# A three-part transformer block on one core: small TensorE operations set singly behind the large matmuls of the next step

## The chip, the cores and the metric

One core of a Trainium2 chip runs the whole program. The metric is the device time of one execution in microseconds (us). The kernel before took 716.36 us, the median of three runs (715.81 to 716.93).

## The reference, cut to what matters

Four batches of 576 positions (2304 tokens in all) go through a windowed attention with eight heads of 64 (four heads see the last 32 positions, four see every fourth of the last 128), then a gated feed-forward layer 512 to 1536 to 512 with an RMS norm ahead, then a second layer 512 to 1024 to 512 with a softmax-weighted activation and a layer norm between its two products.

```python
scores = np.where(masks, scale * q @ k.T, -1e9)
attn = softmax(scores);  x = attn @ v                    # tokens x 512
rms = np.sqrt(np.mean(x * x, axis=-1, keepdims=True) + 1e-06)
xn = x / rms * rms_g
g = xn @ w_gate;  x = (silu(g) * (xn @ w_val)) @ w_out   # 512 -> 1536 -> 512
h = x @ w_in                                             # 512 -> 1024
solu = h * softmax(h)
ln = (solu - mu) / np.sqrt(var + 1e-06) * g_ln
out = ln @ w_out2                                        # 1024 -> 512
```

## The kernel before

**Numbers.** Each operand of a large product is split into a high and a low part, and one product is three matmuls (high by high, high by low, low by high) that add up in PSUM: `mm3` (L909), `product` inside `joint` (L1250), `p_product` (L1565) and `p_products` (L1637). Such a matmul has a stationary side of 128 by 128, loaded by a weight load of its own, and a moving side of 512 columns (256 for one part of the tokens). They are called the large ones here.

**Stages.** The tokens are cut into nine tiles of 256, the tiles into five parts. Attention works through units (one or two groups of heads of a tile): scores, masking, maximum, exponential, sum, division, transposes, the product with v. A unit's 2 or 4 transposes (L662; line L531 for the four earliest units, which the change leaves as they are) turn the weights on TensorE: the data are the stationary side, an identity of 128 columns is the moving side, and the result lands in PSUM, tile `tp`. ScalarE copies it out twice, masked (`turned`, tile `pT`). The mean of the squares for the RMS norm (`mean`, emitted by `total`, L807) is, for the seven later tiles, two matmuls with a moving side of one column; each of these shows in the trace as two. Between all this run the products of the first layer (`g`, `vp`, `out`). From about 315 us the last two parts are done together in Strassen form (`joint`: m1 to m7). From about 500 us the second layer runs, pair r of token tiles by pair: its first product as seven sub-products p1 to p7 (`pair_steps`), then per token tile i of 128 the activation and norm, eight transposes in two sets of four (`p_t`, L1626, PSUM tile `tp`, one bank per set), their split into high and low (`p_lt`: ScalarE casts each set into `lt`, L320; VectorE subtracts, L329), and the product with w_out2 in two halves of twelve matmuls (`p_products`, L1645 to L1647, PSUM tile `o`).

**What sets the order.** Every step is registered with `plan.add`: its engines with an assumed cost, what it needs, what it occupies, and a due time. A list scheduler (`Plan.order`) plays the steps in assumed time and returns one order; the program is emitted in it, so every engine's queue is that list filtered by engine. In the second layer TensorE's order is written out by hand (`line` in `second_stage`): o of tile a first half, transposes of tile b, o of a second half, p2, p7, p4 of the next pair, o of b first half, p3, transposes of the next a, o of b second half, p1, p5, p6 of the pair after. The product p6 adds onto the bank in which p1 left its result, after that result has been copied out (`kept("s1", "p1")`, a copy by ScalarE or VectorE into `h` or `he`). `put` (L318) is the helper behind all copies and casts, `less` (L328) behind all subtractions.

Of the kernel before, what the change touches and what calls it, by code (L numbers as in the profile page):

```python
# [20 lines left out]
P = 128  # L21
KD = DM // P
NF1 = FF1 // P
NF2 = FF2 // P
# [150 lines left out]
    return [("cl" if t == X_ELSEWHERE else "x", x_key(t))]  # L175


class Plan:


# [92 lines left out]
def tile_attention_glu_solu(ctx: ExitStack, tc: tile.TileContext, qk_d, v_d, w1_d, win2_d, wout2_d,  # L273
                            rmsg_d, gln_d, mask_d, ident_d, out):
    nc = tc.nc
# [17 lines left out]
    ident = const.tile([P, P], F32, name="ident")  # L293
# [4 lines left out]
    ones = const.tile([P, P], F32, name="ones")  # L298
# [11 lines left out]
    T = {}  # L310
# [28 lines left out]
                             seed.to_broadcast([P, x.shape[1]]), start=not add, stop=not add)  # L339

    w1 = {}

# [241 lines left out]
    def attention(t, m, due, needs):  # L586
# [3 lines left out]
        g, at_ = gs[0], PLACE[t, ns[0]]  # L590
        K = (t, m)
        w = 512 + g["nk"]
# [64 lines left out]
        def transposes(e):  # L657

            x = new_bank(tp, [P, 4, P], "tp")
            fill(x.rearrange("p u q -> p (u q)"))  # L660
            for u in range(2 * N):
                nc.tensor.transpose(x[:, u], T[s_][:, 2 * u:2 * u + 2, :].rearrange("p r k -> p (r k)"), ident)  # L662

        def turned(r):

# [88 lines left out]
    def rms(t, due, first):  # L754
        p, i = PART_OF[t]
# [45 lines left out]
        def total(k):  # L801

            def emit(e):
                if k == ks[0]:
                    bank(a_mean, [P, 2], "ms")
                for c in range(2):
                    nc.tensor.matmul(T[a_mean][:, c:c + 1], T["sq", t, k][:, P * c:P * c + P], ones[:, 0:1],  # L807
                                     start=k == ks[0] and c == 0 if first else True,
                                     stop=k == ks[-1] and c == 1 if first else True)
            return emit  # L810

        def eps(e):
# [94 lines left out]


    def mm3(acc, wh, wl, xh, xl, first, last):  # L909
        nc.tensor.matmul(acc, wh, xh, start=first, stop=False)  # L910
        nc.tensor.matmul(acc, wh, xl, start=False, stop=False)  # L911
        nc.tensor.matmul(acc, wl, xh, start=False, stop=last)  # L912

    def mlp(v, due):
        p, c0, n, fs = VIRTUAL[v]
# [132 lines left out]
    def joint():  # L1048
# [107 lines left out]
        def group_(q):  # L1156
# [88 lines left out]
            def product(name, a, b, x, more, needs):  # L1245
                def emit(e):
                    for j in range(2):
                        (wh, wl), xu = left(a, j), x_unit(b, j)
                        for n, (w, y) in enumerate(((wh, xu[:, 0]), (wh, xu[:, 1]), (wl, xu[:, 0]))):
                            nc.tensor.matmul(acc(x), w, y, start=not more and j == 0 and n == 0, stop=j == 1 and n == 2,  # L1250
                                             skip_group_check=True)
                add((name, q), {"t": 6 * mm}, emit, needs + lows(b) + ([("slow", q)] if a[0] == "s" else []) +
                    [made[1, f, X] for f in fs], takes=[] if more else [(tag_of[x], bank[x])],
                    uses=[bank[x]] + ([shl] if a[0] == "s" else []) + ([("xt4",)] if b == "t4" else []), due=7000)
# [310 lines left out]
    def p_product(r, a, b, bank, more):  # L1565
        o, yh = p_bank(r, bank), pairs[r]
        for j in range(2):
            x = LEFT[a]
            w = w_in[b, j]
            first, last_ = j == 0 and not more, j == 1  # L1570
            hi = yh[0][x > 2][:, x - 3 * (x > 2), j]
            nc.tensor.matmul(o, hi, w[:, 0], start=first, stop=False, skip_group_check=True)
            nc.tensor.matmul(o, hi, w[:, 1], start=False, stop=False, skip_group_check=True)
            nc.tensor.matmul(o, yh[1][:, x, j], w[:, 0], start=False, stop=last_, skip_group_check=True)

    def p_sum(r, row, col, kept, bank, n):
        if n == 0:
# [42 lines left out]
    def p_t(i, q):  # L1620
        e = flat(p_row(i // 2, ("e", i % 2)))
        tag, n = plan.where["tp", i, q]
        tp = tp_of[i, q] = psy.tile([P, HALF, P], F32, tag=f"{tag}{n}", name="tp")
        for k in range(HALF):
            c = (q * HALF + k) * P
            nc.tensor.transpose(tp[:, k, :], e[:, c:c + P], ident)  # L1626

    def p_lt(i, q, h, e):
        if i not in lt_of:
# [7 lines left out]
    def p_products(i, ks, a=0, n=DM):  # L1637
        lt = lt_of[i]
        if (i, a) not in o_of:
            tag, x = plan.where["o", i, a]  # L1640
            o_of[i, a] = psy.tile([P, 512], F32, tag=f"{tag}{x}", name="o")[:, 0:n]
        o = o_of[i, a]
        for k in ks:
            w = w1[OUT_AT[k]][:, :, a:a + n]
            nc.tensor.matmul(o, lt[:, 0, k], w[:, 0], start=(k == 0), stop=False)  # L1645
            nc.tensor.matmul(o, lt[:, 0, k], w[:, 1], start=False, stop=False)  # L1646
            nc.tensor.matmul(o, lt[:, 1, k], w[:, 0], start=False, stop=(k == NF2 - 1))  # L1647

    rows = [(PIECES[t][j][0] * S + PIECES[t][j][1], PIECES[t][j][2])
            for p in PARTS for t in p for j in range(len(PIECES[t]))]  # L1650
# [180 lines left out]
    nc.scalar.activation(early, mhalf[:, 0:1], AF.Exp)  # L1831
    with tc.manual_schedule():
        free, warm = 0.0, ps.tile([P, TP], F32, tag="vp0", name="warm")
        for at_, _, name, e in plan.play():
            if e == "t":
                filling[0] = int((at_ - free) / (0.13 if free else 0.25)) if at_ < FILL else 0
                free = at_ + plan.steps[name]["engines"]["t"]
                if name[0] == "spread":
                    warm = None
                if warm is not None:  # L1840
                    fill(warm)
            plan.steps[name]["emit"](e)


def _layout(q, k, v):
# [69 lines left out]
```

## Time and profile before

| | |
|---|---|
| median of three runs | 716.36 us |
| the profiled execution | 717.14 us, of which the profile's span is 715.1 us |
| TensorE busy | 706.7 us (99% of the span) |
| TensorE weight loads | 597.1 us (83%) |
| VectorE, ScalarE, GpSimd busy | 485.6, 361.8, 125.7 us |
| granted TensorE clock, mean | 0.997 |

The span runs from the first to the last recorded instruction; 2.0 us of the profiled execution lie outside it. PE is TensorE's matmuls, PEld its weight loads, DVE is VectorE, ACT is ScalarE. A matmul's recorded length holds its way through the array, so matmuls that follow closely overlap in the record: what a matmul costs the queue is the distance from its start to the next one's, not its length.

### The profile page before, as it was taken

To read this page: it belongs to the slowest core of one execution; us is meant where nothing else is said; L and a number is where in the kernel's file an instruction comes from. 1 tells how busy PE (TensorE), PEld (TensorE's weight loads), DVE (VectorE), ACT (ScalarE), POOL (GpSimd) and SP (SyncE) were. 2 spreads that over 40 slices of the span, in tenths; PEclk is the share of its full clock that TensorE was granted. 3 is DMA by queue.
4 is the path that set the end of the run, shared out by engine and by line. 5 is a ranking of instruction groups with operands and counts; after the bars stand their busy time and mean duration, and the time that the engine had idled before them with its cause. 6 is when DMAs were issued, how large, how long until landed. Compare 5 with 4: busy or idle time off the path is not lost.

```text
span 715.1 us, 11752 instructions
## 1 busy us (share of the span) xinstructions
PE 706.7 (99%) x4561; PEld 597.1 (83%) x4561; DVE 485.6 (68%) x891; ACT 361.8 (51%) x775; POOL 125.7 (18%) x159
## 2 busy tenths in 40 slices
PE   8999999999999999999999999999999999999998
PEld 5788888899998888888888888888778888888887
DVE  4798897478657665367766666689677676665552
ACT  2877835354435563335555554355365555443440
POOL 0323033232312211110000000014044411001110
PEclk9999999999999999999999999999999999999999
DMA  9999323173278837204211112846032111000001
GB/s 325 402 408 345 135 85 136 60 235 125 103 257 296 290 118 215 94 30 143 93 44 44 60 58 91 321 161 223 0 118 74 59 61 45 29 16 31 29 30 45
DMA packets 42423, 97.22 MB, mean 136 GB/s; under 512 B 3840, under 2 KB 14080, under 8 KB 42368
## 3 DMA queue, kind: packets, MB, share of 16 engines
q1 hardware_dynamic: 40640, 93.33, 37.4%
q10 hardware_dynamic: 1728, 3.15, 1.2%
q8 instruction: 36, 0.59, 0.4%
q14 instruction: 19, 0.16, 0.1%
HBM read 72.87 MB, written 23.59 MB: 135 GB/s over the span
## 4 chain that ended last, share of the span: by engine, by line
PE 88%; DVE 4%; DMA 4%; issue 1%; ACT 1%; POOL 1%; SPq 1%; DVEq 0%; ACTq 0%; POOLq 0%
PE ca L1250 7%; PE y L910 5%; PE y L912 5%; PE y L911 5%; PE o L1647 5%; PE o L1645 5%; PE o L1646 5%; PE g L910 4%; PE vp L910 4%; PE g L911 4%; PE vp L912 4%; PE g L912 4%; PE vp L911 4%; PE pv L682 2%; PE cd L1250 2%; PE cc L1250 2%
## 5 line engine op out<-in xcount | busy, mean ns | idle before, releaser
L1645 PE MATMUL o<-w,lt 128*128 128x512 f32 (+1 forms) x152 | 58.9, 388 | 0.0
L1647 PE MATMUL o<-w,lt 128*128 128x512 f32 (+1 forms) x152 | 57.6, 379 | 0.0
L1646 PE MATMUL o<-w,lt 128*128 128x512 f32 (+1 forms) x152 | 57.5, 379 | 0.0
L329 POOL TENSOR_TENSOR w<-wf,w 128x512 fp32r<-128x512 f32 (+1 forms) x12 | 19.8, 1658 | 196.4 <-ACT w L320 196.4
L910 PE MATMUL y<-uh,w 128*128 128x512 f32 (+1 forms) x148 | 53.7, 363 | 0.0
L912 PE MATMUL y<-uh,w 128*128 128x512 f32 (+1 forms) x148 | 51.8, 350 | 0.0
L911 PE MATMUL y<-uh,w 128*128 128x512 f32 (+1 forms) x148 | 51.7, 349 | 0.0
L647 ACT ACTIVATE s<-s,nm 128x64 f32<-128x64 f32 x120 | 40.1, 336 | 20.4 <-DVE nm L642 20.4
L944 ACT ACTIVATE u<-g 128x512 f32<-128x512 f32 (+1 forms) x37 | 19.1, 516 | 46.6 <-PE g L912 46.5
L792 POOL TENSOR_TENSOR sq<-x 128x256 f32<-128x256 f32 x28 | 19.7, 713 | 127.2 <-DVE x L324 65.4
L910 PE MATMUL g<-xh,w 128*128 128x512 f32 (+1 forms) x104 | 40.6, 390 | 0.0
L910 PE MATMUL vp<-xh,w 128*128 128x512 f32 (+1 forms) x100 | 39.4, 394 | 0.0
L320 ACT CAST w<-wf 128x512 fp32r<-128x512 f32 (+1 forms) x40 | 28.3, 727 | 21.2 <-DVE wf L382 8.8
L911 PE MATMUL g<-xl,w 128*128 128x512 f32 (+1 forms) x104 | 38.9, 374 | 0.0
L912 PE MATMUL g<-xh,w 128*128 128x512 f32 (+1 forms) x104 | 38.9, 374 | 0.0
L912 PE MATMUL vp<-xh,w 128*128 128x512 f32 (+1 forms) x100 | 38.2, 382 | 0.0
L911 PE MATMUL vp<-xl,w 128*128 128x512 f32 (+1 forms) x100 | 38.1, 381 | 0.0
L954 DVE SCALAR_TENSOR_TENSOR u<-u,vp 128x512 f32<-128x512 f32 (+1 forms) x37 | 21.7, 586 | 22.2 <-PE vp L912 21.4
L320 ACT CAST uh<-u 128x512 fp32r<-128x512 f32 (+1 forms) x37 | 19.8, 536 | 28.8 <-DVE u L954 28.5
L950 DVE SCALAR_TENSOR_TENSOR u<-u,g 128x512 f32<-128x512 f32 (+1 forms) x37 | 21.6, 584 | 17.5 <-ACT u L944 17.1
L1647 PEld LDWEIGHTS o<-w,lt 128*128 128x128 f32 x152 | 28.6, 188 | 5.4
L1645 PEld LDWEIGHTS o<-w,lt 128*128 128x128 f32 x152 | 28.6, 188 | 4.8
(284 smaller groups left out, 2017.8 us busy)
## 6 DMA issues: line engine op xcount, KB each, us to landing
raw<-w SPq DMA_DIRECT2D x36, 512.0 KB, 9.1
es<-ec SPq DMA_DIRECT2D x12, 512.0 KB, 3.3
sc<-es SPq DMA_DIRECT2D x12, 512.0 KB, 3.3
qk<-qk SPq DMA_DIRECT2D x7, 800.0 KB, 5.9
vt<-v SPq DMA_DIRECT2D x10, 512.0 KB, 5.1
wo<-w SPq DMA_DIRECT2D x9, 512.0 KB, 8.6
wst<-wo SPq DMA_DIRECT2D x9, 512.0 KB, 3.7
yT<-yo SPq DMA_DIRECT2D x16, 256.0 KB, 3.5
```

The source lines that it names most:

```text
L320: nc.scalar.copy(dst, src) if scale is None else nc.scalar.mul(dst, src, scale)
L329: ENG[e].tensor_tensor(dst, a, b, ALU.subtract)
L647: nc.scalar.activation(T[s_][:, i], T[s_][:, i], AF.Exp, bias=st["nm"][:, i:i + 1], accum_out=sm[:, i:i + 1])
L910: nc.tensor.matmul(acc, wh, xh, start=first, stop=False)
L911: nc.tensor.matmul(acc, wh, xl, start=False, stop=False)
L912: nc.tensor.matmul(acc, wl, xh, start=False, stop=last)
L950: return lambda e: nc.vector.scalar_tensor_tensor(out=u_of(f), in0=u_of(f), scalar=1.0, in1=T["g", v, f], op0=ALU.add, op1=ALU.mult)
L954: return lambda e: nc.vector.scalar_tensor_tensor(out=u_of(f), in0=u_of(f), scalar=0.5, in1=T["vp", v, f], op0=ALU.mult, op1=ALU.mult)
L1250: nc.tensor.matmul(acc(x), w, y, start=not more and j == 0 and n == 0, stop=j == 1 and n == 2, skip_group_check=True)
L1645: nc.tensor.matmul(o, lt[:, 0, k], w[:, 0], start=(k == 0), stop=False)
L1646: nc.tensor.matmul(o, lt[:, 0, k], w[:, 1], start=False, stop=False)
L1647: nc.tensor.matmul(o, lt[:, 1, k], w[:, 0], start=False, stop=(k == NF2 - 1))
```

## The change

A transpose step and a mean step no longer issue their matmuls. They put them on a list (`small_ones`), and each large matmul of the next TensorE step takes one from the list and issues it right behind itself (`large`). What is left at the end of that step is issued then (`flush`). Only the steps named in `LARGE` take small ones; ahead of any other TensorE step the list is emptied. When a step of another engine that needs a listed step comes up in the plan's order first, the next TensorE step is pulled ahead of it, or, if that step isn't a large one or isn't ready, the list is emptied. The plan itself, its costs and due times are as before.

```diff
--- before
+++ changed
@@ -175,6 +175,10 @@
     return [("cl" if t == X_ELSEWHERE else "x", x_key(t))]
+WEAVE = ("t", "transposes", "mean")
+LARGE = ("g", "vp", "out", "o") + tuple(f"{x}{n}" for x in "mp" for n in range(1, 8))
+
+
 class Plan:
@@ -340,6 +344,21 @@
+    pending, woven = [], set()
+
+    def small_ones(*fs):
+        pending.extend(fs)
+
+    def flush():
+        while pending:
+            pending.pop(0)()
+        woven.clear()
+
+    def large(*args, **more):
+        nc.tensor.matmul(*args, **more)
+        if pending:
+            pending.pop(0)()
+
     w1 = {}
     def prepare(stage, f, cuts, srcs, scales, dues, needs=(), lead=((1, 0), "joined", 0)):
@@ -659,7 +678,8 @@
             x = new_bank(tp, [P, 4, P], "tp")
             fill(x.rearrange("p u q -> p (u q)"))
             for u in range(2 * N):
-                nc.tensor.transpose(x[:, u], T[s_][:, 2 * u:2 * u + 2, :].rearrange("p r k -> p (r k)"), ident)
+                y = T[s_][:, 2 * u:2 * u + 2, :].rearrange("p r k -> p (r k)")
+                small_ones(lambda u=u, y=y: nc.tensor.transpose(x[:, u], y, ident))
         def turned(r):
@@ -804,9 +824,11 @@
                 if k == ks[0]:
                     bank(a_mean, [P, 2], "ms")
                 for c in range(2):
-                    nc.tensor.matmul(T[a_mean][:, c:c + 1], T["sq", t, k][:, P * c:P * c + P], ones[:, 0:1],
-                                     start=k == ks[0] and c == 0 if first else True,
-                                     stop=k == ks[-1] and c == 1 if first else True)
+                    x, y = T[a_mean][:, c:c + 1], T["sq", t, k][:, P * c:P * c + P]
+                    if first:
+                        nc.tensor.matmul(x, y, ones[:, 0:1], start=k == ks[0] and c == 0, stop=k == ks[-1] and c == 1)
+                    else:
+                        small_ones(lambda x=x, y=y: nc.tensor.matmul(x, y, ones[:, 0:1], start=True, stop=True))
             return emit
         def eps(e):
@@ -907,9 +929,9 @@
     def mm3(acc, wh, wl, xh, xl, first, last):
-        nc.tensor.matmul(acc, wh, xh, start=first, stop=False)
-        nc.tensor.matmul(acc, wh, xl, start=False, stop=False)
-        nc.tensor.matmul(acc, wl, xh, start=False, stop=last)
+        large(acc, wh, xh, start=first, stop=False)
+        large(acc, wh, xl, start=False, stop=False)
+        large(acc, wl, xh, start=False, stop=last)
     def mlp(v, due):
         p, c0, n, fs = VIRTUAL[v]
...
@@ -1569,9 +1591,9 @@
             w = w_in[b, j]
             first, last_ = j == 0 and not more, j == 1
             hi = yh[0][x > 2][:, x - 3 * (x > 2), j]
-            nc.tensor.matmul(o, hi, w[:, 0], start=first, stop=False, skip_group_check=True)
-            nc.tensor.matmul(o, hi, w[:, 1], start=False, stop=False, skip_group_check=True)
-            nc.tensor.matmul(o, yh[1][:, x, j], w[:, 0], start=False, stop=last_, skip_group_check=True)
+            large(o, hi, w[:, 0], start=first, stop=False, skip_group_check=True)
+            large(o, hi, w[:, 1], start=False, stop=False, skip_group_check=True)
+            large(o, yh[1][:, x, j], w[:, 0], start=False, stop=last_, skip_group_check=True)
     def p_sum(r, row, col, kept, bank, n):
         if n == 0:
@@ -1623,7 +1645,7 @@
         tp = tp_of[i, q] = psy.tile([P, HALF, P], F32, tag=f"{tag}{n}", name="tp")
         for k in range(HALF):
             c = (q * HALF + k) * P
-            nc.tensor.transpose(tp[:, k, :], e[:, c:c + P], ident)
+            small_ones(lambda k=k, c=c: nc.tensor.transpose(tp[:, k, :], e[:, c:c + P], ident))
     def p_lt(i, q, h, e):
         if i not in lt_of:
...
@@ -1831,7 +1853,20 @@
     nc.scalar.activation(early, mhalf[:, 0:1], AF.Exp)
     with tc.manual_schedule():
         free, warm = 0.0, ps.tile([P, TP], F32, tag="vp0", name="warm")
-        for at_, _, name, e in plan.play():
+        todo, emitted = plan.play(), set()
+
+        def needs_of(name):
+            return set(plan.steps[name]["needs"])
+
+        while todo:
+            at_, _, name, e = todo[0]
+            if woven & (needs_of(name) - plan.steps[name]["after"]):
+                at_, _, name, e = next(y for y in todo if y[3] == "t")
+                if name[0] not in WEAVE + LARGE or needs_of(name) - emitted:
+                    flush()
+                    at_, _, name, e = todo[0]
+            todo.remove(next(y for y in todo if y[2] == name))
+            emitted.add(name)
             if e == "t":
                 filling[0] = int((at_ - free) / (0.13 if free else 0.25)) if at_ < FILL else 0
                 free = at_ + plan.steps[name]["engines"]["t"]
@@ -1839,7 +1874,13 @@
                     warm = None
                 if warm is not None:
                     fill(warm)
+                if name[0] not in WEAVE + LARGE:
+                    flush()
             plan.steps[name]["emit"](e)
+            if e == "t" and name[0] in WEAVE and pending:
+                woven.add(name)
+            elif e == "t":
+                flush()
 def _layout(q, k, v):
```

The order of VectorE, ScalarE, GpSimd and the DMA queue stays what it was, row for row. On TensorE the 204 transposes of L662 and L1626 and the 14 mean matmuls stood in runs of 2, 4 or 8; of them 201 transposes and all 14 means now stand singly behind a large matmul (187 and 10 behind one with 512 columns, the rest behind one with 256), and one run of three transposes is left.

TensorE in the second layer, before: the eight transposes (`tp`, two banks) of one token tile stand between p3 of a pair (`hb`) and the second half of o of the tile ahead.

```order
L1574 MATMUL hb_5398<-w0_1_449,yh_5291 128x512
L1626 MATMUL tp_5489<-ident_83,e_5304 128x128 x4
L1626 MATMUL tp_5496<-ident_83,e_5304 128x128 x4
L1645 MATMUL o_5457<-w3_2_875,lt_5366 128x512
L1646 MATMUL o_5457<-w3_2_875,lt_5366 128x512
L1647 MATMUL o_5457<-w3_2_875,lt_5366 128x512
L1645 MATMUL o_5457<-w6_1_1060,lt_5366 128x512
```

The same place in the changed kernel, from the last matmuls of p3 on (line L358 is now the one line of all large matmuls, L1648 the transposes).

```order
L358 MATMUL hb_5398<-w0_1_449,yh_5291 128x512 x3
L358 MATMUL o_5457<-w3_2_871,lt_5378 128x512
L1648 MATMUL tp_5489<-ident_83,e_5296 128x128
L358 MATMUL o_5457<-w3_2_871,lt_5378 128x512
L1648 MATMUL tp_5489<-ident_83,e_5296 128x128
L358 MATMUL o_5457<-w3_2_871,lt_5378 128x512
L1648 MATMUL tp_5489<-ident_83,e_5296 128x128
L358 MATMUL o_5457<-w6_1_1060,lt_5378 128x512
L1648 MATMUL tp_5489<-ident_83,e_5296 128x128
L358 MATMUL o_5457<-w6_1_1060,lt_5378 128x512
L1648 MATMUL tp_5492<-ident_83,e_5296 128x128
L358 MATMUL o_5457<-w6_1_1060,lt_5378 128x512
```

The transposes of the second bank now start behind the fifth large matmul of the half, and the last of them stands behind the eighth of its twelve.

ScalarE at this place, in the changed kernel: `lt` are the two casts of the transposed sets, `yh` a cast for the next pair, `sq` a square of the norm, `ob` the scaled result of an earlier tile, `h` the copy of p1's result (and after it one more).

```order
L324 CAST yh_5490<-y_5394 128x768
L324 CAST lt_5514<-tp_5489 128x512
L324 CAST lt_5514<-tp_5492 128x512
L324 CAST yh_5490<-y_5394 128x1024
L1626 ACTIVATE sq_5523,st_5317<-e_5296,st_5317 128x1024
L324 ACTIVATE ob_5533<-o_5457,st_5156 128x512
L324 COPY h_5545<-ha_5525 128x512 x2
```

Nothing moved here: the kernel before has the same rows in the same order (its helper is line L320, its square L1604).

TensorE at the mean of one tile in the first layer, before: `ms` are the two mean matmuls, in front of the second half of a `vp` product.

```order
L912 MATMUL vp_1344<-xh_460,w9_0_1258 128x512
L807 MATMUL ms_1352<-ones_88,sq_970 128x1 x2
L910 MATMUL vp_1344<-xh_460,w9_0_1258 128x512
L911 MATMUL vp_1344<-xl_465,w9_0_1258 128x512
L912 MATMUL vp_1344<-xh_460,w9_0_1258 128x512
```

And in the changed kernel.

```order
L358 MATMUL vp_1344<-xh_460,w9_0_1258 128x512 x2
L831 MATMUL ms_1352<-ones_88,sq_970 128x1
L358 MATMUL vp_1344<-xl_465,w9_0_1258 128x512
L831 MATMUL ms_1352<-ones_88,sq_970 128x1
L358 MATMUL vp_1344<-xh_460,w9_0_1258 128x512 x2
```

The two means are one large matmul apart, and the first stands one large matmul later than it did.

## Rows read from the trace of the kernel before

**Rows 1.** The page's first part (busy time, share, instructions) and its clock row.

```profile
PE 706.7 (99%) x4561; PEld 597.1 (83%) x4561; DVE 485.6 (68%) x891; ACT 361.8 (51%) x775; POOL 125.7 (18%) x159
...
PEclk9999999999999999999999999999999999999999
```

**Rows 2.** Groups by line and shape on PE: busy us, mean ns of one.

```profile
L1626 PE MATMUL tp<-ident,he 128*128 128x128 f32 x80 | 10.4, 272 | 0.0
...
L662 PE MATMUL tp<-ident,s 128*128 128x128 f32 x60 | 9.2, 273 | 0.0
L1626 PE MATMUL tp<-ident,e 128*128 128x128 f32 x64 | 8.3, 272 | 0.0
```

**Rows 3.** Timeline of PE, one run of eight transposes: start, length, instruction.

```profile
560.31 0.40 PE L1647 MATMUL o<-w,lt 128*128 128x512 f32 x1
560.55 1.04 PE L1626 MATMUL tp<-ident,e 128*128 128x128 f32 x8
561.34 0.48 PE L1645 MATMUL o<-w,lt 128*128 128x512 f32 x1
561.65 0.40 PE L1646 MATMUL o<-w,lt 128*128 128x512 f32 x1
...
562.34 0.39 PE L1646 MATMUL o<-w,lt 128*128 128x512 f32 x1
...
565.97 0.39 PE L1574 MATMUL ha<-w,yl 128*128 128x512 f32 x1
```

**Rows 4.** Timeline of the weight loads in the same stretch.

```profile
560.31 1.03 PEld L1626 LDWEIGHTS tp<-ident,e 128*128 128x128 f32 x8
561.31 0.19 PEld L1645 LDWEIGHTS o<-w,lt 128*128 128x128 f32 x1
561.42 0.19 PEld L1646 LDWEIGHTS o<-w,lt 128*128 128x128 f32 x1
```

**Rows 5.** Timeline of PE, a run of four transposes in the first layer.

```profile
105.67 0.39 PE L912 MATMUL vp<-xh,w 128*128 128x512 f32 x1
105.90 0.60 PE L662 MATMUL tp<-ident,s 128*128 128x128 f32 x4
```

**Rows 6.** Timeline of PE, the matmuls of one mean.

```profile
116.77 0.50 PE L807 MATMUL ms<-ones,sq 128*128 128x1 f32 x4
```

**Rows 7.** Timeline of the weight loads behind that mean.

```profile
117.11 0.19 PEld L910 LDWEIGHTS vp<-xh,w 128*128 128x128 f32 x1
```

**Rows 8.** Timeline of PE, large matmuls with 256 columns.

```profile
162.97 0.28 PE L910 MATMUL y<-uh,w 128*128 128x256 f32 x1
...
163.57 0.28 PE L912 MATMUL y<-uh,w 128*128 128x256 f32 x1
```

**Rows 9.** Timeline of PE, one turn of the second layer: transposes, then p6's first matmul.

```profile
550.13 1.03 PE L1626 MATMUL tp<-ident,e 128*128 128x128 f32 x8
...
556.46 0.39 PE L1572 MATMUL ha<-w,w 128*128 128x512 f32 x1
```

**Rows 10.** Timeline of ACT in that turn; in brackets its idle time and what ended it.

```profile
551.11 1.07 ACT L320 CAST lt<-tp 128x512 fp32r<-128x512 f32 x2
...
554.16 0.69 ACT L320 ACTIVATE ob<-o,st 128x512 f32<-128x512 f32 x1
555.29 0.59 ACT L320 COPY h<-ha 128x512 f32<-128x512 f32 x1 [0.45 <-PE ha L1574]
```

**Rows 11.** Timeline of PE, the transposes of the last such turn.

```profile
661.13 1.04 PE L1626 MATMUL tp<-ident,he 128*128 128x128 f32 x8
```

**Rows 12.** Timeline of ACT in the last such turn.

```profile
661.76 1.07 ACT L320 CAST lt<-tp 128x512 fp32r<-128x512 f32 x2 [2.20 <-PE tp L1626]
...
666.29 0.59 ACT L320 COPY he<-ha 128x512 f32<-128x512 f32 x1 [0.61 <-PE ha L1574]
```

**Rows 13.** Timeline of ACT, the copies of one attention unit.

```profile
140.09 1.27 ACT L320 ACTIVATE pT<-tp,half 128x512 f32<-128x512 f32 x2 [0.46 <-PE tp L662]
```

**Rows 14.** Timeline of PE, that unit's product with v.

```profile
142.07 1.15 PE L682 MATMUL pv<-pT,vt 128*64 128x64 f32 x32
```

More of the change, by code (lines that the diff above doesn't have):

```diff
@@ L1249, in emit @@
                         for n, (w, y) in enumerate(((wh, xu[:, 0]), (wh, xu[:, 1]), (wl, xu[:, 0]))):
-                            nc.tensor.matmul(acc(x), w, y, start=not more and j == 0 and n == 0, stop=j == 1 and n == 2,
+                            large(acc(x), w, y, start=not more and j == 0 and n == 0, stop=j == 1 and n == 2,
                                              skip_group_check=True)
@@ L1644, in p_products @@
             w = w1[OUT_AT[k]][:, :, a:a + n]
-            nc.tensor.matmul(o, lt[:, 0, k], w[:, 0], start=(k == 0), stop=False)
-            nc.tensor.matmul(o, lt[:, 0, k], w[:, 1], start=False, stop=False)
-            nc.tensor.matmul(o, lt[:, 1, k], w[:, 0], start=False, stop=(k == NF2 - 1))
+            large(o, lt[:, 0, k], w[:, 0], start=(k == 0), stop=False)
+            large(o, lt[:, 0, k], w[:, 1], start=False, stop=False)
+            large(o, lt[:, 1, k], w[:, 0], start=False, stop=(k == NF2 - 1))
     rows = [(PIECES[t][j][0] * S + PIECES[t][j][1], PIECES[t][j][2])
```

## The prediction

> **What bounds the kernel now.** I read the page's first part and its clock row first, then the groups by line on TensorE, then the timeline around runs of transposes, matmuls and weight loads apart, and last the timeline of ScalarE behind them. TensorE's matmuls are busy 99% of the span, and the granted clock is full in almost every slice (the higher of its two levels, 2.4 GHz) [rows 1]. So the kernel's time is the sum of what its matmuls cost TensorE's queue, and a change pays if that sum gets smaller or a wait of TensorE goes. The operations moved are 144 transposes in the second layer and 60 in attention [rows 2], and 14 mean matmuls. By the groups they look dear (272 ns each), but that is a recorded length, and what counts is the distance between starts.
>
> That distance is read at a run of eight [rows 3]. Large matmuls follow each other 0.227 us apart (562.34 to 565.97, 16 steps). From the large one ahead of the run (560.31) to the fifth behind it (562.34) pass 2.03 us; five steps without transposes would be 1.13. So eight transposes cost 0.90 us, 0.112 each. The weight loads show why [rows 4]: a load starts when the matmul just ahead of it starts, never earlier, and the load of the first large matmul behind the run starts at 561.31, with the eighth transpose; the next load, which marks that large matmul's true start, comes at 561.42. Eight transposes from 560.55 to 561.31 are seven steps of 0.109, and from the last one to the large matmul there are again 0.11.
>
> The means tell what the 0.11 is [rows 6, 7]: four matmuls that stream one column still stand 0.113 apart (116.77 to 117.11, three steps). Where nothing streams, the load alone sets the step, some 0.11 us. A large matmul hides the load behind it; a short one doesn't.
>
> The Trainium skill, in "TensorE: Matmul & The Clock Gate", section "Step-by-step: what each phase is for", says that TensorE's queue pulls weight loads ahead of matmuls in flight, with the matmuls in order. Here the trace agrees so far as one load ahead, and shows none two matmuls ahead.
>
> **The transposes.** In the changed kernel a pair is large, transpose, large. Its two gaps both occur in the trace already. Large to transpose is 0.24 in the second layer [rows 3] and 0.23 in attention [rows 5]; transpose to large is 0.11 [rows 4]. The transpose's own load is now always hidden, but the load of the next large matmul is always exposed: in a run of eight there are eight exposed loads (seven transposes' and one large one's), and singly there are eight exposed loads of large ones. Together 0.34 to 0.35 less the 0.227 of the large one: 0.113 to 0.123 per transpose, against 0.112. At the upper end the slightly longer step after a run (561.42 to 561.65 is 0.23) now comes every time, 0.005 more: 0.128. At the lower end a switch costs nothing, 0.227 + 0.109, so 0.109. So per transpose between 0.003 less and 0.016 more, times 201: -0.6 to +3.2 us. I take the middle, 0.006 more, since both switch distances were measured above the plain step: +1.2 us. The means have the same balance; two runs of two in place of one of four pay the switch twice, about 0.03 us for each of seven tiles: +0.2.
>
> **What becomes late.** A transpose set is ready later, because large matmuls stand between its members. In the second layer the queue behind that is ScalarE's, and its order is unchanged: two casts of the set, a cast for the next pair, a square, a scaled result, and then the copy of p1's result, for which p6 on TensorE waits. Before, the eight transposes begin at 550.13 [rows 9] and the last is done at 550.13 + 0.76 + 0.27, 551.16; ScalarE starts the first cast at 551.11 and the second half a length later, at about 551.6 [rows 10]. Now the large matmul takes the place at 550.13, the first transpose follows at 550.36, the eighth seven pairs of 0.34 later at 552.75, done at 553.03. The second cast starts at 553.1, 1.5 us later, and everything behind it on ScalarE with it. The cover is ScalarE's idle time ahead of the copy, 0.45 us, and the distance from the copy's end, 555.88, to p6's start at 556.46, 0.58 [rows 9, 10]: 1.03 in all. So p6 starts some 0.5 us late and TensorE stands still for that long. In the last such turn the transposes begin at 661.13 [rows 11], so the eighth is done at 664.03; the second cast stood at about 662.25, is 1.8 late, and finds 0.61 idle and the same 0.58 ahead of p6 [rows 12]: 0.6. There are six such turns, 22.2 us apart (550.13 to 661.13 are five of them) [rows 9, 11]; in five the copy is ScalarE's, in one VectorE's, whose queue I find covered. Five times 0.5 to 0.65 is 2.7 us. Bounds: if a part of the delay is made up, 0.2 each, 1 us; if each wait is 0.9, as when the whole 1.5 meets only the 0.58, 4.5 us. I take 2.7, since its terms are single rows.
>
> In attention a unit's fourth transpose ends some 0.9 us later in a stream of 512 columns (three more large matmuls and one ahead), half of that with 256. The copies behind it [rows 13] end at 141.36 and the product with v starts at 142.07 [rows 14], 0.71 ahead; the other units are alike or wider. That gives a wait of a few tenths in two or three units. Against it, a transpose now waits for its input one large matmul later, which saves as much where VectorE is the late one. I cost this at +0.1 us, between -0.4 and +1.
>
> Nothing moves on the DMA queues or on GpSimd, and no wait of another engine is added.
>
> **The sum.** 1.2 + 0.2 + 2.7 + 0.1 = 4.2 us. The profiled execution of before took 717.1 us, its span 715.1 with 2.0 around it; it would become 721.3. The median of the runs is 0.8 below the profiled one, so the forecast is 716.4 + 4.2, about 720.5 us.
>
> **The rivals.**
> First, the small ones dearer singly. A run of eight pays 0.90 - 8 x 0.109, about 0.025 us, beyond its steps; if every transpose pays all of that by itself, each costs 0.021 more than now, 201 of them 4.2 us, and with the waits (3.0) the time is 723.6. For it: the step is longer for more than one large matmul after a run. Against it: in the new order the next transpose comes before those later steps.
>
> Second, the waits don't come: ScalarE gains the delay back between the second cast and the copy. Then only the 1.2 + 0.2 stay, 717.8 us. For it: ScalarE is busy only 51% [rows 1]. Against it: in these turns it is idle only 0.45 to 0.61 us behind the casts [rows 10, 12].
>
> Third, on the other side: the transpose hides. If 0.109 in a run is the transposes' own loading, and behind a large matmul a transpose occupies the array only for its columns, it costs little. Large matmuls with 256 columns stand 0.12 apart (162.97 to 163.57, five steps) [rows 8] and with 512 columns 0.227, so 128 columns are worth 0.053 and a transpose 0.053 + 0.013, 0.066: 0.046 less than now, 201 times, 9.2 us saved, against 3.0 of waits: 710.2 us. The point from which it decides is the gap from a transpose to the large matmul behind it: below about 0.095 us the kernel gets faster in spite of the waits. That gap stands in the trace, at the end of every run, at 0.11, and the means show a load alone at the same size.
>
> The Trainium skill's page "TensorE: Matmul & The Clock Gate", section "Back-to-back issue gap", speaks for this rival: 128 columns at full clock cost 56 ns back to back. By that, as an estimate, the saving would be 201 x 0.056 = 11 us and the time about 708. The trace differs: runs stand at 109 ns.
>
> That the change doesn't do what it says is excluded by the order: only three of 204 transposes are left in a run.
>
> **How the numbers follow.** The forecast (waits at p6, small switches) gets 62%, with its own range 719 to 722.5; the first rival 15%, the second 16%, the third 7%. The range reaches from just below the second rival to the first: 717.3 to 723.6. 0.2% of 716.4 is 1.4 us, about what a measurement of this kernel can tell from no change: faster is under 714.9, slower over 717.8. The second rival sits on that edge; I give 11% to the same and 7% to faster, the rest, 82%, to slower.
>
> **What would show it.** In the profile after: transposes singly, 0.34 to 0.35 us from large to large across one; a load ahead of the next large matmul that starts with the transpose. ScalarE's second cast of a set 1.5 to 1.8 us later within its turn, no idle time ahead of the copy of p1's result in five turns, and PE idle of about 0.5 us at p6 (`ha`) waiting for ScalarE, where before it has none. It would be wrong if large-to-large across a transpose is under 0.32 us, or if p6 starts without a wait.

## The result, and the profile after

The kernel became slower by 0.7%: 721.90 us, the median of 6 runs, against 716.44 for the kernel before on the same chip; the ratio is 1.0069, with a 95% interval of 1.0057 to 1.0080. The profiled execution took 722.4 us and its span is 720.4, against 717.1 and 715.1 before: 5.3 us more. Nearly all of it lies on TensorE's queue, whose last matmul starts 5.2 us later than before. First the page's opening part, which answers to [rows 1]:

```profile
PE 711.3 (99%) x4561; PEld 593.6 (82%) x4561; DVE 487.8 (68%) x891; ACT 361.8 (50%) x775; POOL 125.0 (17%) x159
...
PEclk9999999999999999999999999999999999999999
```

The groups by line and shape on TensorE that answer to [rows 2] (last columns: busy us, mean ns of one, idle time ahead):

```profile
L1648 PE MATMUL tp<-ident,he 128*128 128x128 f32 x80 | 21.3, 271 | 0.0
L1648 PE MATMUL tp<-ident,e 128*128 128x128 f32 x64 | 17.3, 271 | 0.0
L682 PE MATMUL tp<-ident,s 128*128 128x128 f32 x60 | 15.9, 271 | 0.0
```

The instructions are as many as before and the granted clock is full. The transposes' busy time doubles (10.4 to 21.3 us in the first group) while the mean of one stays 271 ns: alone, a transpose's recorded length no longer overlaps that of the next one. That is why the cost isn't read from this column, but from the starts. The timeline of TensorE in the turn of [rows 9]:

```profile
551.68 0.39 PE L358 MATMUL o<-w,lt 128*128 128x512 f32 x1
551.92 0.27 PE L1648 MATMUL tp<-ident,e 128*128 128x128 f32 x1
551.94 0.48 PE L358 MATMUL o<-w,lt 128*128 128x512 f32 x1
552.26 0.27 PE L1648 MATMUL tp<-ident,e 128*128 128x128 f32 x1
...
554.33 0.27 PE L1648 MATMUL tp<-ident,e 128*128 128x128 f32 x1
554.36 1.17 PE L358 MATMUL o<-w,lt 128*128 128x512 f32 x4
555.36 0.62 PE L358 MATMUL ha<-w,w 128*128 128x512 f32 x2
...
557.86 0.39 PE L358 MATMUL hb<-w,yl 128*128 128x512 f32 x1
558.42 0.73 PE L358 MATMUL ha<-w,w 128*128 128x512 f32 x2 [0.18 <-ACT h L324]
558.99 0.40 PE L358 MATMUL ha<-w,yl 128*128 128x512 f32 x1
```

Transposes stand 0.345 us apart (551.92 to 554.33, seven steps), one large matmul between each two: 0.118 more than the plain step of 0.227. From 551.68 to 555.36 are twelve large steps and eight transposes, 3.68 - 12 x 0.227 = 0.96 for the set, against 0.90 in [rows 3]. Counted up to the twelfth large matmul behind each set it is 0.97 in thirteen of the eighteen sets, and 0.94 to 1.02 in the others.

At 558.42 stands what the forecast named: p6's first matmul waits for ScalarE's copy `h`. From 557.86 it stands 0.56 behind, where 0.227 is the step, and the next step is 0.34 (the first two are one row; the third, at 558.99, is 0.57 behind the first, and 0.23 of that is its own step): 0.33 + 0.11 lost. The timeline of ScalarE there answers to [rows 10]:

```profile
553.27 0.59 ACT L324 CAST lt<-tp 128x512 fp32r<-128x512 f32 x1 [0.51 <-PE tp L1648]
554.64 0.59 ACT L324 CAST lt<-tp 128x512 fp32r<-128x512 f32 x1 [0.78 <-PE tp L1648]
...
557.22 0.68 ACT L324 ACTIVATE ob<-o,st 128x512 f32<-128x512 f32 x1
557.79 0.58 ACT L324 COPY h<-ha 128x512 f32<-128x512 f32 x1
```

The two casts, back to back before, now each wait for TensorE, and the 0.45 idle ahead of the copy is gone. Such a wait stands in five turns (558.42, 603.59, 626.38, 649.17, 672.14), 0.42 to 0.45 us in four of them and 0.6 in the last: 2.3 in all.

In attention the jump is at one unit. First TensorE's timeline, where the product with v answers to [rows 14], then SyncE's queue of loads (`pv` is the product with v, `sp` the scores, `rs` a matmul that spreads the factors of the norm over the partitions and needs VectorE's `rd`):

```profile
142.66 1.15 PE L702 MATMUL pv<-pT,vt 128*64 128x64 f32 x32 [0.17 <-ACT pT L324]
...
151.95 1.15 PE L645 MATMUL sp<-qk 128*64 128x64 f32 x32 [0.54 <-DMA qk<-qk]
...
154.91 0.67 PE L849 MATMUL rs<-rd,ones 128*128 128x256 f32 x2 [0.19 <-DVE rd L844]
```

```profile
143.85 0.34 SPq L632 DMA_DIRECT2D vt<-v  x1
144.31 0.76 SPq L626 DMA_DIRECT2D qk<-qk  x1
```

The product with v waits for ScalarE's casts, 0.27 us by the shift of its line; the load of the next q and k goes out behind it; and the scores, nine microseconds later, wait for that load. Against the kernel before, the same large matmuls stand 0.31 us later just ahead of the unit's transposes at 139.5 and 1.79 later at 156.

### The profile page after: what moved, and what is told of

Same layout as the page of the kernel before. It is cut to its first block, busy times and chain, and to the rows that moved or that the text cites. A ratio compares the mean times of both kernels' runs of the same rounds, so it can differ in the third digit from the quotient of the medians.

```text
span 720.4 us, 11750 instructions
## 1 busy us (share of the span) xinstructions
PE 711.3 (99%) x4561; PEld 593.6 (82%) x4561; DVE 487.8 (68%) x891; ACT 361.8 (50%) x775; POOL 125.0 (17%) x159
## 3 DMA queue, kind: packets, MB, share of 16 engines
q10 hardware_dynamic: 1728, 3.15, 1.2%
## 4 chain that ended last, share of the span: by engine, by line
PE 90%; DMA 4%; ACT 3%; DVE 2%; issue 1%; SPq 0%; POOL 0%; ACTq 0%; DVEq 0%; POOLq 0%
PE y L358 19%; PE o L358 14%; PE g L358 11%; PE vp L358 11%; PE ca L358 7%; PE ha L358 4%; PE hb L358 2%; PE cd L358 2%; PE cc L358 2%; PE ce L358 2%; PE cb L358 2%; PE pv L702 2%; PE tp L1648 2%; PE sp L645 2%; DMA raw<-w 2%; PE hc L358 2%
## 5 line engine op out<-in xcount | busy, mean ns | idle before, releaser
L358 PE MATMUL o<-w,lt 128*128 128x512 f32 (+1 forms) x456 | 118.0, 405 | 0.0
L358 PEld LDWEIGHTS o<-w,lt 128*128 128x128 f32 x456 | 81.1, 188 | 20.2 <-DVE lt L333 0.2
L358 PE MATMUL y<-uh,w 128*128 128x512 f32 (+1 forms) x444 | 95.5, 358 | 0.0
L358 PEld LDWEIGHTS y<-uh,w 128*128 128x128 f32 x444 | 72.8, 189 | 11.5
L358 PE MATMUL g<-xh,w 128*128 128x512 f32 (+1 forms) x208 | 67.2, 383 | 0.0
L358 PE MATMUL vp<-xh,w 128*128 128x512 f32 (+1 forms) x200 | 66.3, 390 | 0.0
L358 PE MATMUL y<-w,w 128*128 128x512 f32 x216 | 49.9, 389 | 0.0
L358 PEld LDWEIGHTS y<-w,w 128*128 128x128 f32 x216 | 40.5, 188 | 8.4
L358 PEld LDWEIGHTS g<-xh,w 128*128 128x128 f32 x208 | 38.4, 189 | 7.2
L333 DVE TENSOR_TENSOR lt<-tp,lt 128x512 fp32r<-128x512 f32 x36 | 24.7, 690 | 28.7 <-ACT lt L324 28.7
L358 PEld LDWEIGHTS vp<-xh,w 128*128 128x128 f32 x200 | 37.1, 188 | 7.3
L324 ACT CAST lt<-tp 128x512 fp32r<-128x512 f32 x36 | 21.0, 586 | 43.3 <-PE tp L1648 43.1
L358 PE MATMUL g<-xl,w 128*128 128x512 f32 (+1 forms) x104 | 39.5, 380 | 0.0
L358 PE MATMUL vp<-xl,w 128*128 128x512 f32 (+1 forms) x100 | 39.3, 393 | 0.0
```

The lines of the kernel that those rows point to most:

```text
L324: nc.scalar.copy(dst, src) if scale is None else nc.scalar.mul(dst, src, scale)
L333: ENG[e].tensor_tensor(dst, a, b, ALU.subtract)
L358: nc.tensor.matmul(*args, **more)
```

## The experiments

Two numbers describe each run. "Median" is the change against the kernel before, timed alternately on the same chip (ratio and 95% interval; 0.001 is 0.72 us). "Attention" and "second layer" compare one profiled execution with that of before: how much longer the way is from the large matmul at 60 us to the one at 500, and from the one at 515 to the last one, at 711.6. In the parts that a kernel left alone these were -0.23 to +0.26 in attention and -0.73 to +0.07 in the second layer, mostly by one wait of p-products for VectorE at 530 us, which was 0.7 in the execution of before and 0 to 0.8 in others.

| run | median | attention | second layer |
|---|---|---|---|
| the change | 1.0069 [1.0057, 1.0080] | +1.82 | +3.15 |
| second layer alone | 1.0058 [1.0045, 1.0071] | -0.10 | +3.19 |
| attention and means alone | 1.0015 [1.0005, 1.0024] | +1.83 | +0.07 |
| the same again | 1.0020 [1.0010, 1.0029] | +1.04 | -0.73 |
| run of eight, late | 1.0046 [1.0034, 1.0058] | -0.23 | +2.93 |
| pairs, second layer | 1.0001 [0.9992, 1.0010] | -0.10 | +0.33 |
| second layer, p2 ahead of p6 | 1.0017 [1.0008, 1.0026] | +0.26 | +1.16 |
| p2 ahead of p6 alone | 1.0003 [0.9994, 1.0012] | -0.08 | -0.16 |
| run of eight behind the first large | 1.0003 [0.9995, 1.0012] | +0.18 | -0.58 |
| attention, one unit in a run | 1.0007 [0.9998, 1.0015] | +0.76 | -0.27 |
| that one unit alone | 1.0014 [1.0005, 1.0023] | +0.64 | -0.42 |
| the change, both waits covered | 1.0028 [1.0016, 1.0039] | +0.69 | +1.44 |
| the same in pairs | 1.0016 [1.0007, 1.0025] | +0.17 | +0.18 |

Theory A: the cost is mostly lateness (a set's last transpose comes later, and a product behind it waits). Theory B: it is the standing singly itself. The two runs on a long landing, further down, have theories of their own.

**The two halves.** First the second layer alone, with attention's transposes and the means in runs:

```
-WEAVE = ("t", "transposes", "mean")
+WEAVE = ("t",)
-                small_ones(lambda u=u, y=y: nc.tensor.transpose(x[:, u], y, ident))
+                nc.tensor.transpose(x[:, u], y, ident)
```

> Only the 144 transposes of the second layer are put singly behind large matmuls; attention's transposes and the means stand in runs as before. Theory A (the cost is two things, a few ns per single transpose and the late copy of p1's result in five turns of the second layer, the rest of the change costing some 2 us in attention): +3 to +3.5 us on before, PE waits of 0.3 to 0.6 us at p6 in five turns, 2.3 us together. Rival B (every single small matmul is simply dearer, wherever it stands, and the waits only take up time that TensorE would have lost anyway): the whole change's 5 us shared by the count of transposes, 144 of 201, +3.6 us. Rival C (the cost arises in attention, where a later copy makes later loads): under +1.5 us.

Then the other half, line 1648 as a plain transpose again:

> Only attention's 60 transposes and the 14 means are put singly; the second layer's transposes stand in runs as before. Theory A: +1.2 to +1.9 us (singles about 0.5, a wait of the product with v for its copy near 142 us about 0.3, and what follows it up to 155 us; less if the wait for the load of the next unit's q and k at 152 us doesn't come again). Rival B: 57 of 201 of 5 us, +1.4 us, spread evenly over 64 to 315 us. Rival C: +3.5 us or more.

The halves add up: 0.58% and 0.15% to 0.69%. The second layer came out a little above what was expected, with the waits at p6 of the same size as in the full change. It carries over three quarters. Attention came out at 1.1 us by the median, just under what A expected. By size these two runs exclude only rival C, since A and B expect nearly the same of either half. The place tells more: in attention the jump of 1.49 us at one unit stands again, out of 1.83, where rival B has the cost spread evenly.

**Late but not single.** The second layer's eight transposes stay a run, issued behind the eighth large matmul of the following step:

```
         nc.tensor.matmul(*args, **more)
-        if pending:
-            pending.pop(0)()
+        since[0] += 1
+        if pending and since[0] == 8:
+            while pending:
+                pending.pop(0)()
```

> Second layer only: the eight transposes of a set stay in a run, but the run is issued behind the eighth large matmul of the step (behind the sixth and last of p4 in the first turn), so that they are as late as in the change without being single. Theory A: the waits at p6 come as in the change, 2.3 us in five turns, no cost of singles, and the transposes behind p4 fill a wait of 0.6 us that TensorE has there before: +1.7 us, between +1.2 and +2.3. Rival B (the singles are the cost): -0.6 to 0 us.

It cost 3.4 us (2.4 to 4.2), above the range of A, and far from B. Its timeline of TensorE:

```profile
551.76 1.04 PE L1650 MATMUL tp<-ident,e 128*128 128x128 f32 x8
...
556.65 0.73 PE L358 MATMUL ha<-w,w 128*128 128x512 f32 x2 [0.22 <-ACT h L324]
```

The run is as dense as in [rows 3], and p6 waits all the same, in the same five turns, 0.49 to 0.68 us each, 2.7 in all, where A had 2.3. So lateness is enough by itself. In the control the run is moved as well, but behind the first large matmul (`== 1` in place of `== 8`), 0.23 us later than before:

> Second layer: the run of eight transposes stays a run, but is issued behind the first large matmul of the following step instead of ahead of it: moved, 0.23 us late, not single. Theory A: the eighth transpose is 0.23 us later than before, which the slack ahead of p6 (0.45 us idle and 0.58 between the copy's end and p6) covers, so no waits: -0.3 to +0.4 us. Theory B: as before too. A cost of 2 us or more would say that moving transposes into another step costs by itself, whatever their place.

No change, and no wait at p6: moving into another step costs nothing while the set stays within the 1.03 us of cover.

**Single but less late.** Two transposes behind each large matmul (`for _ in range(2)` around the `if pending`) in the second layer:

> Second layer only: two transposes behind each large matmul instead of one, so that a set is complete after four large matmuls: half as late, in pairs. Theory A: the eighth transpose is done some 0.9 us later than in a run, under the 1.03 to 1.2 us of cover, so no wait at p6; of the cost of singles about half: +0.4 to +0.9 us. Rival B: half of the second layer's cost, +1.8 us.

```profile
549.79 0.39 PE L358 MATMUL o<-w,lt 128*128 128x512 f32 x1
550.02 0.38 PE L1649 MATMUL tp<-ident,e 128*128 128x128 f32 x2
...
551.51 2.09 PE L358 MATMUL o<-w,lt 128*128 128x512 f32 x8
...
556.18 0.62 PE L358 MATMUL ha<-w,w 128*128 128x512 f32 x2
```

The set is done a microsecond earlier than singly, p6 starts without a wait, and nothing measurable is left by the median (+0.1 us, -0.6 to +0.7; the upper part of that lies in the range of A). The trace still has a price: a set cost 0.93 to 0.95 us here, against 0.90 in a run.

**Single and late, but covered.** Transposes singly in the second layer, and p2's six large matmuls put ahead of p6 on TensorE:

```
-            line += h(r, "p1", "p5", "p6") * (q > 0) + ...
+            line += h(r, "p1", "p5", "p2", "p6") * (q > 0) + ...
-                (... if q == 0 else h(r, "p2", "p7", "p4"))
+                (... if q == 0 else h(r, "p7", "p4"))
```

> Second layer alone woven, as in the run with that half alone (+4.1 us), but on TensorE p2's matmuls of the same turn are put between p5 and p6, where they stood behind p6 before: six large matmuls, 1.36 us more between the set's transposes and the product that waits for ScalarE's copy. Nothing is less single and no cast is earlier. Theory A (the late copy that p6 waits for makes the cost): no wait of ha on ScalarE in the five turns, TensorE's line 0.45 to 0.6 us shorter in each, so the kernel before +0.8 to +1.3 us, which is what the single transposes cost by themselves less the wait at 530 that they fill. Theory B (transposes standing singly make the cost): +3.5 to +4, as without the move. If between, some other product has become the late one.

> Control for the run with p2 ahead of p6: the kernel before, its transposes in runs, with p2 moved the same way and nothing woven. Both theories: no wait was there to be covered, so no change, -0.5 to +0.5 us. If it is faster or slower, the move itself has a price, and the other run is read against this one.

```profile
557.71 0.39 PE L358 MATMUL hc<-w,yl 128*128 128x512 f32 x1
557.94 0.61 PE L358 MATMUL ha<-w,w 128*128 128x512 f32 x2
```

p6 follows p2 by the plain step, without a wait, in all five turns. The cost fell from 4.1 us to 1.2 by the medians, as A said; the move itself changes nothing. This is the cleanest test: the same transposes, as single and as late, with two thirds of the cost gone.

**The unit in attention.** The half with attention and means, with the transposes of the one unit at 139.5 us in a run:

```
+ (small_ones if K != (3, 1) else lambda f: f())(lambda u=u, y=y: nc.tensor.transpose(x[:, u], y, ident))
```

> Attention's transposes and the means woven (that half alone gave +1.1 us by the medians, +1.9 in its profiled execution), except that one unit's four transposes, at 139.5 us, are left in a run. Theory A (one late product with v there frees its buffers late, the next unit's load is issued late, and the scores then wait for the DMA): the wait of pv for the casts at 142, the scores' wait for the DMA at 152 and the wait for VectorE behind it vanish; the profiled execution is 0.5 to 0.7 us above the one of before, and the median 0 to +0.5. Rival (many small costs all over attention, singleness and means): at most 0.1 less than without this edit, and the jump of 1.4 us between 140 and 156 stays.

```profile
141.94 1.15 PE L702 MATMUL pv<-pT,vt 128*64 128x64 f32 x32
...
150.49 1.10 PE L645 MATMUL sp<-qk 128*64 128x64 f32 x32
```

All three waits vanished, and the jump with them (0.01 us between 140 and 156, where it was 1.49). But one part of the expectation doesn't hold. A late load can't by itself make the scores late, since both follow the same product: from the issue of the load to the scores are 6.9 us before (143.73 to 150.62). What differs is how long the load takes from issue to landing. The group of the load of q and k in the view of transfers between 142 and 152.5 us, of the kernel before and of the changed one (KB, us to landing):

```profile
qk<-qk SPq DMA_DIRECT2D x1, 928.0 KB, 5.2
```

```profile
qk<-qk SPq DMA_DIRECT2D x1, 928.0 KB, 7.6
```

So the last two runs asked whether the long landing comes with the late product: this one unit singly and nothing else (`K == (3, 1)`), and the half with attention a second time.

> The kernel before, with the four transposes of one attention unit (the one at 139.5 us) put singly behind large matmuls, and nothing else. The load of the next q and k took 7.6 us from issue to landing in the two executions so far in which that unit's product with v waits for the casts, and 5.0 to 7.0 us in the ten others; what stands between its issue and the scores that need it is some 6.9 to 7.1 us in all of them, since both follow that product. Theory A (the long transfer comes with the late product): pv waits 0.2 at 142, the load lands after some 7.6, the scores wait about 0.5 for it, rs waits behind it, 1.2 to 1.7 us by 156, and the median +0.6 to +1.3. Theory B (the length of the transfer is that execution's own): pv waits 0.2 to 0.3 and no more than that, 0.3 to 0.4 us by 156, and the median 0 to +0.5; a landing of 5 to 7 us.

> The kernel with only attention's transposes and the means singly once more: a second execution's trace of the same program, and more times. Theory A (the long transfer comes with the late product): again a landing of about 7.6 us, the scores waiting some 0.5 us for it at 152, and +1.2 to +1.9 us. Theory B (it was that execution's own): a landing of 5 to 7 us, no such wait, +0.3 to +0.4 at 156 and 0.5 to 1.0 us over the whole span; the median between +0.5 and +1.1 by either.

The wait of the product for the casts came back in both, 0.27 us as before. The landing took 6.8 and 7.2 us, between the two theories; the scores waited for it only in the run with the whole half.

```profile
142.47 1.15 PE L702 MATMUL pv<-pT,vt 128*64 128x64 f32 x32 [0.17 <-ACT pT L324]
...
151.00 1.10 PE L645 MATMUL sp<-qk 128*64 128x64 f32 x32
```

Over all executions the landing took 6.8, 7.2, 7.6 and 7.6 us in the four with the late product, and 5.0 to 7.0 in the ten others. It tends to be longer behind a late product, but the two overlap. Why is open: no run changed what else those transfers meet. Steady is the 0.27. On top, by the shift of TensorE's line, the scores came 0 to 0.75 late and `rs` behind them 0 to 0.46. These two are not of the late product alone: with the unit in a run they are 0 in eight of ten executions, but 0.21 and 0.17 in the run with p2 ahead of p6, and 0.02 and 0.36 in the run of eight behind the first large matmul, neither of which touches attention. The one unit alone cost 0.14% by the median, the other fifteen sets and the means together 0.07% (0.0 to 0.15).

**Both covered.** The full change with p2 ahead of p6 and the one unit in a run, and the same with two small ones behind each large matmul:

> The whole change (+5.3 us in its profiled execution), with both late places covered: on TensorE p2's matmuls between p5 and p6 in the second layer, and the one unit's transposes at 139.5 us in attention left in a run. 200 transposes and the 14 means still stand singly. Theory A (the two late places are the whole rest): the costs of the two halves with their waits covered add up, 1.2 and 0.5, so +1.2 to +2.3 us by the medians, some 718.4, and neither a wait of ha for ScalarE nor one of sp for the DMA. Theory B (small ones are dear singly, or the halves hurt each other): +3 or more.

> As the run with both late places covered, but two small ones behind each large matmul in place of one: half as many switches, and a set's last transpose some 0.7 us earlier. Theory A (what is left there is the price of a switch from large to small and back, and of the slower steps behind a woven set): half of the rest or less, -0.3 to +1.0 us against the kernel before. Rival (the rest is lateness that shows in no wait): nearer to the run with singles, +1.2 or more.

The first cost 0.28%, the second 0.16%, with no wait of `ha` for ScalarE in either; by the profiled parts 2.1 and 0.35 us. The first is as A said. The second stands at 1.1 us by the median (0.5 to 1.8), a little above the range of A and a little below that of its rival, and inside A's by the profile: it doesn't decide between them. No version was faster than the kernel before.

## Why the prediction was right, and where it wasn't

The forecast was 720.5 us, slower, with waits at p6 as the main term; it came to 721.9, inside its own range.

- **A transpose costs the same singly, and slightly more.** Right in kind. Large to large across one transpose is 0.345, within the 0.34 to 0.35 forecast, because the load of the next large matmul is now exposed each time. The weight loads of the changed kernel show it, answering to [rows 4]:

```profile
551.92 0.19 PEld L358 LDWEIGHTS o<-w,lt 128*128 128x128 f32 x1
552.05 0.14 PEld L1648 LDWEIGHTS tp<-ident,e 128*128 128x128 f32 x1
552.26 0.19 PEld L358 LDWEIGHTS o<-w,lt 128*128 128x128 f32 x1
```

  The large matmul's load starts with the transpose, at 551.92, and the next transpose's load, which marks the large one's start, at 552.05: 0.13 from transpose to large, above the 0.095 from which the third rival would have decided. The excess over the run was 0.07 per set of eight (0.97 against 0.90), 1.3 us for eighteen, and 0.035 per set of four behind 512 columns (0.490 against 0.455), 0.4 for eleven: 1.7, where 1.2 was forecast. The term was sized from the steps next to a transpose; the steps behind a whole set are slower too. The first rival had the direction, a price for each switch, but 0.021 us for it, where 0.009 was measured.
- **The waits at p6.** Right in place, number and releaser. The second cast was forecast at 553.1 in the turn of before; it stands at 554.64, and the turn itself starts 1.55 later (551.68 against 550.13), so counted from the turn of before that is 553.1. Five waits made 2.3 us, forecast 2.7. The run with p2 ahead of p6 takes them away, and 2.9 us of time by the medians.
- **Attention.** This term was mis-sized: +0.1 forecast, within -0.4 to +1. Half the mechanism was there (0.71 us of slack, a wait of a few tenths), but the sum set it against a saving that doesn't occur, and stopped at the product with v. What is queued behind that product, the load of the next q and k, was not followed. "Nothing moves on the DMA queues" and "no wait of another engine is added" hold for the program's order, not for its times: the load goes out 0.58 us later (144.31 against 143.73), and in that execution the scores wait for it. The wait and what comes behind it made 1.5 us in the profiled execution of the change, 0.7 in a second one of the same half; that one unit alone cost 1.0 us by the median (0.4 to 1.6). Only 0.27 of it came in every execution with the unit singly.
- **The means** were forecast at +0.2. No run took them alone; with the fifteen sets that don't wait they cost 0.5 us by the median (-0.1 to +1.1). The traces put them near nothing: one mean behind 512 columns lengthens the line by 0.476 us singly, 0.472 before, counted to the fourth large matmul behind it.
- **The sum** was 4.2 and is 5.3 by the profiled executions, 5.5 by the medians: the waits 0.4 under, the means 0.2 under, the singles 0.5 over, attention about 1.4 over. Of the second layer 1.3 + 2.3 would be 3.6, and its part is 3.15: the wait for VectorE at 530, 0.7 in the execution of before, isn't there in that of the changed kernel. The transposes stand in it, but an execution with that layer in runs lacked it too, so it is not put down to the change. Another 0.3 us lie outside the two parts of the table. That the sum comes within 1.3 us is in part luck: this wait, which is no term of it, and the two terms that came out small took back 1.3 of the 1.9 us by which attention and the singles were over.
- **The third rival** fell with the 0.345. The Trainium skill's "TensorE: Matmul & The Clock Gate", section "Back-to-back issue gap", gives 56 ns for 128 columns, but as the gap of a matmul without its weight load, and about 81 ns where each matmul has a weight load of its own, as here; the prediction took the 56 without that condition. Behind a large matmul a transpose added 118 ns here, more than the 112 in a run, so neither figure is reached in either place.
- **The reading of the loads.** "Never earlier" holds in the trace of before for every load of a full 128 by 128. About half of the loads of the scores and of the product with v, which are 128 by 64, start 0.05 us ahead of the matmul before them; nothing in the sum rests on those.

## What to carry to other kernels

A short matmul put behind a long one hides its own weight load and exposes that of the next long one: count loads that nothing long covers, on both sides, before counting on overlap. Spreading a set over the work that follows makes its last member late by the length of all that stands between, so look at what is queued behind the set on the reading engine, and how much idle time stands ahead of the first result that TensorE needs from it; here 1.03 us was enough for pairs and not for singles. A wait that looks small can cost more than its own length: follow what is issued behind it, loads above all.

## What was not expected of the hardware

- The large matmuls behind most sets of singles stay slow for up to a dozen steps: a set's excess grows from 0.932 us right behind it to 0.950 four large ones on and 0.973 twelve on, then stands still. Behind a run it goes from 0.891 to 0.900 within four.
- A wait costs about 0.11 us beyond itself: the matmul behind the waiting one stands 0.34 from it in place of 0.227, at all five waits (558.42 to 558.76 is one). The weight loads show what that is: the load of the waiting matmul had itself waited for the copy and starts with it, so nothing hides it.

```profile
558.42 0.30 PEld L358 LDWEIGHTS ha<-w,w 128*128 128x128 f32 x2 [0.60 <-ACT h L324]
```

- A transfer of 928 KB in the same place of the program took 5.0 to 7.6 us to land, over fourteen executions; why is open.
